# Identity products on TensorE beside the conversion of the first layer's weights, in a fused kernel of top-k attention and two gated layers

## The chip, the cores and the metric

One Trainium2 chip, one of its cores. The metric is the device time of one execution of the program in microseconds, the median of several runs. Five engines take part, each with its own row of instructions that it works off in order: TensorE (PE, with its weight loads as PEld), VectorE (DVE), ScalarE (ACT), GpSimd (POOL), and SyncE (SP), whose row here holds the DMA issues.

## The reference

Attention over 4 x 8 heads of 576 tokens with head size 64, in which each row keeps its 32 largest scores, and behind it two layers on the 2304 tokens of width 512.

```python
scores = scale * np.matmul(q, k.transpose(0, 1, 3, 2))
kth = np.partition(scores, -top_k, axis=-1)[..., -top_k:-top_k + 1]
scores = np.where(scores >= kth, scores, -1000000000.0)
attn = softmax(scores)                                   # 1e-09 is added to the sum
x = np.matmul(attn, v)                                   # heads joined: 2304 x 512
gate = 1.0 / (1.0 + np.exp(-(x @ w_gate)))               # 512 x 1536
x = gate * (x @ w_val) @ w_out                           # 512 x 1536, 1536 x 512
r = np.maximum(x @ w_in, 0.0)                            # 512 x 2048
out = (r * r) @ w_out2                                   # 2048 x 512
```

q, k and v come as float32, the five weights as float64.

## The kernel before

**Tiles.** The 2304 tokens are 18 tiles of 128 rows, grouped in chunks: six of one tile, then six of two. For each chunk the attention of eight heads is computed in units of one head and one tile: scores on PE (line 374), copied out of PSUM by ACT (377), the 32nd largest found by DVE in four rounds of MAX8 and MATCH_REPLACE8 (389, 396), the masked exponentials on ACT (408, 424). The first two chunks then go on in float32: PE transposes the exponentials with a product against a diagonal (472, 483), ACT copies them out (475, 484), PE multiplies with the values (533).

**Weights.** [...] A matrix is cut into blocks of 128 x 512, 12 for each of w_gate, w_val and w_out (wg, wv, wo) and 16 for each of the second layer's (wi, w2). `conv` (586 to 628) takes two blocks at a time: ACT copies the high words (607), DVE shifts them (609), ACT scales the low words (613), the sign comes from DVE (620) or, for one pair in three, from a pass of ACT (616), and POOL adds the low part (623). `scale` (630) sums the squares of a matrix on PE (the gram products of line 640) and derives a power of two from it, and `split` (654) cuts the float32 weight into two float16 ones.

**Layers.** Chunks 0 and 1 run through both layers in float32 (`moe32`, 895): pairs of 128-column slices go through the gate's product and tanh (905, 914), POOL's scaling of it (915), DVE's product g (917), and the accumulation with wo on PE (927), later the second layer (952, 969). All later chunks use three float16 products for one float32 one (`moe_head` and `moe`, lines 747, 787, 851, 872).

**Order.** Nothing of the engines' rows is written out. The program gives each instruction a priority, and a planner that has times of its own for the instructions sets the rows ahead of the run. The loop at 1188 to 1226 gives the weight steps, attention units and layer steps of the first two chunks their due times (`at`, 1167), so that conversion, attention and float32 layers are interleaved. An added instruction can therefore move others, on all engines. A row's instruction waits by semaphores for its inputs and for its buffers, and what stands behind it on its engine waits with it.

**PSUM.** Four pools share its eight banks: ps_s (scores, two banks), ps_t (transposes, two), ps_w (layer products, two) and ps_a (accumulators, two). The first accumulator of the layers is allocated at line 922.

Of the kernel before, what the change touches and what calls it, by code (L numbers as in the profile page):

```python
# [10 lines left out]
F32 = mybir.dt.float32  # L11
# [3 lines left out]
AF = mybir.ActivationFunctionType  # L15
# [3 lines left out]
NOSYNC = mybir.DependencyInfo(mybir.DependencyClass.NoSync, mybir.DependencyReason.DATA)  # L19
DRAM = bass.MemoryType.DRAM  # L20

P = 128
# [22 lines left out]
XP = (0, 1)  # L45
CN = 16
CA2 = 5.0
SM2 = ()
XUP = 1000
DIAG = 2  # L50
# [24 lines left out]
def tile_topk_attention__then__two_moe_layers(  # L75
# [14 lines left out]
    nc = tc.nc  # L90
# [25 lines left out]
    ps_a = ctx.enter_context(tc.tile_pool(name="ps_a", bufs=2, space=PSUM))  # L116
    ps_w = ctx.enter_context(tc.tile_pool(name="ps_w", bufs=2, space=PSUM))

    ident = const.tile([P, P], F32, name="ident")
# [446 lines left out]
    def fetch_to(i):  # L566
        while fetched[0] < len(blocks):
            b = fetched[0]
            spare = b >= len(blocks) - M4RAW
            if b > i and not (b <= i + PREF and (spare or live[0] + 3 <= WSLOTS)):  # L570
                break
            n, kt, fb = blocks[b]
            src = weights[n][kt * P : (kt + 1) * P, fb * 512 : (fb + 1) * 512]
            pool, kw = (mpool, {"tag": "m4", "bufs": M4}) if spare else (wpool, {"tag": "w"})
            if src.dtype == F32:
                t = pool.tile([P, 512], F32, name=f"{n}_r{kt}_{fb}", **kw)
                nc.sync.dma_start(t, src)
            else:
                t = pool.tile([P, 512, 2], U32, name=f"{n}_r{kt}_{fb}", **kw)
                nc.sync.dma_start(t.rearrange("p f t -> p (f t)"), src.bitcast(U32))  # L580
            if not spare:
                live[0] += 1
            raws[(n, kt, fb)] = t
            fetched[0] += 1

    def conv(name, pi):

        pr = pairs_of[name][pi]
        fetch_to(blocks.index((name, *pr[-1])))
        if (name, pi) in CM4:  # L590
            c = mpool.tile([P, 2, 512], F32, tag="m4", bufs=M4, name=f"{name}_c{pi}")
        else:
            c = wpool.tile([P, 2, 512], F32, tag="w", name=f"{name}_c{pi}")
            live[0] += 1
        rs = [raws.pop((name, kt, fb)) for kt, fb in pr]
        ci = c.bitcast(U32)
        wide = weights[name].dtype != F32
        for e, r in enumerate(rs):
            nblk[0] += 1
            if not wide:  # L600
                nc.gpsimd.tensor_copy(c[:, e], r)
            elif YMOD and nblk[0] % YMOD == 0:
                nc.gpsimd.tensor_scalar(
                    c[:, e], r.bitcast(F32)[:, :, 1], REBIAS, 1.0, op0=ALU.mult, op1=ALU.mult
                )
            else:
                nc.scalar.activation(c[:, e], r.bitcast(F32)[:, :, 1], AF.Copy, scale=REBIAS)
        if wide:
            nc.vector.tensor_scalar(ci, ci, 3, None, op0=ALU.logical_shift_left)
            for e, r in enumerate(rs):  # L610
                hi = r[:, :, 1]
                low = r[:, :, 0].bitcast(I32)
                nc.scalar.activation(low, r[:, :, 0], AF.Copy, scale=float(2.0**-29))
                if nblk[0] // 2 % SGN in SGNS:

                    nc.scalar.activation(
                        r.bitcast(F16)[:, :, 1], hi.bitcast(F32), AF.Copy, scale=float(2.0**-60)
                    )
                else:
                    nc.vector.scalar_tensor_tensor(  # L620
                        ci[:, e], hi, 0x80000000, ci[:, e], op0=ALU.bitwise_and, op1=ALU.bitwise_or
                    )
                nc.gpsimd.tensor_tensor(
                    c.bitcast(I32)[:, e], c.bitcast(I32)[:, e], low, op=ALU.add
                )
        live[0] -= sum(blocks.index((name, *b)) < len(blocks) - M4RAW for b in pr)
        for e, (kt, fb) in enumerate(pr):
            flat[(name, kt, fb)] = (c, e)
# [42 lines left out]
    def weight_step(n=1):  # L671
        for _ in range(min(n, len(steps) - nstep[0])):
            name, pi = steps[nstep[0]]
            conv(name, pi)
            nstep[0] += 1
# [328 lines left out]
    def attention():  # L1004
# [62 lines left out]
        def tail(n, after=None):  # L1067
# [3 lines left out]
            if pr.hp == 0 and pr.ci not in xts:  # L1071
# [10 lines left out]
                else:  # L1082

                    small = pr.ci in SM2
                    x = mpool.tile(
# [102 lines left out]
    for ci in PLAIN:  # L1188
        n = 0
        while True:  # L1190
# [29 lines left out]
            else:  # L1220
                at(ta)
                with tc.high_priority(offset=0):
                    if next(att, 1) is None:
                        emitted[0] += 1
                ta += CA if emitted[0] < CN else CA2
        body = None
# [56 lines left out]
```

## Time and profile before

| | us |
|---|---|
| median of 3 runs | 1274.77 (1273.74 to 1278.67) |
| profiled execution | 1270.1 |
| its span, first to last instruction | 1267.8 |
| PE busy in the span | 1171.9 (92%) |
| DVE busy | 956.3 (75%) |
| ACT busy | 830.0 (65%) |
| POOL busy | 844.9 (67%) |

Mean granted clock of TensorE over the span: 0.966. The shares are means over stages with different limits: in the first eighth of the span ACT and DVE are nearly full and PE has gaps, later PE is nearly full, and from about 960 us on it is almost the only busy engine. So a stage has to be read by itself: in which of its parts which engine has no idle time, and what an engine that waits is waiting for.

### The profile page before, as it was taken

To read this page: it belongs to the slowest core of one execution; us is meant where nothing else is said; L and a number is where in the kernel's file an instruction comes from. 1 tells how busy PE (TensorE), PEld (TensorE's weight loads), DVE (VectorE), ACT (ScalarE), POOL (GpSimd) and SP (SyncE) were. 2 spreads that over 40 slices of the span, in tenths; PEclk is the share of its full clock that TensorE was granted. 3 is DMA by queue.
4 is the path that set the end of the run, shared out by engine and by line. 5 is a ranking of instruction groups with operands and counts; after the bars stand their busy time and mean duration, and the time that the engine had idled before them with its cause. 6 is when DMAs were issued, how large, how long until landed. Compare 5 with 4: busy or idle time off the path is not lost.

```text
span 1267.8 us, 30670 instructions
## 1 busy us (share of the span) xinstructions
PE 1171.9 (92%) x11477; PEld 952.5 (75%) x11477; DVE 956.3 (75%) x1965; ACT 830.0 (65%) x1719; POOL 844.9 (67%) x1294
## 2 busy tenths in 40 slices
PE   6657889999889989899998999999999999999998
PEld 5436877987777868779786778877886887787775
DVE  6998789899789868889997788998999969210010
ACT  4998996577676766667766676776676757322122
POOL 1788774488776576777875887797688749515223
PEclk9667999999989999999997999999999999999999
DMA  6988763223354346665667465466544623200000
GB/s 183 366 293 284 259 191 85 57 78 88 109 151 118 95 93 147 147 134 119 146 128 155 99 164 120 119 138 154 105 101 92 126 48 67 55 1 1 18 1 17
DMA packets 243188, 153.92 MB, mean 121 GB/s; under 512 B 193120, under 2 KB 209504, under 8 KB 243040
## 3 DMA queue, kind: packets, MB, share of 16 engines
q1 hardware_dynamic: 243040, 151.97, 47.1%
q8 instruction: 90, 1.47, 0.5%
q14 instruction: 58, 0.48, 0.1%
HBM read 105.51 MB, written 18.09 MB: 97 GB/s over the span
## 4 chain that ended last, share of the span: by engine, by line
PE 62%; DVE 14%; ACT 9%; DMA 7%; POOL 5%; issue 3%; SPq 1%; DVEq 0%; POOLq 0%; ACTq 0%
PE ph L851 11%; PE acc L872 10%; PE pv L747 7%; PE pg L747 7%; PE acc L787 6%; PE sp L374 6%; DVE mx L389 5%; DVE W L396 5%; PE xp L506 2%; PE ph L952 2%; DMA PT<-S 2%; DMA kst<-ks 2%; PE acc L969 2%; PE xp L533 2%; PE qpt L334 1%
## 5 line engine op out<-in xcount | busy, mean ns | idle before, releaser
L389 DVE MAX8 mx<-W 128x8 f32<-128x576 f32 x432 | 327.9, 759 | 11.1
L396 DVE MATCH_REPLACE8 W<-mx,W 128x576 f32<-128x576 f32 x288 | 213.8, 742 | 0.0
L851 PE MATMUL ph<-x,wi_w 128*128 128x256 f16 (+1 forms) x1920 | 190.7, 252 | 4.6 <-ACT x L825 3.6
L872 PE MATMUL acc<-w_w,rh 128*128 128x512 f16 x768 | 181.8, 379 | 2.2 <-POOL rh L864 2.2
L851 PEld LDWEIGHTS <-wi_w 128*128 128x128 f16 x1920 | 156.4, 98 | 30.6 <-issue 5.2
L747 PE MATMUL pv<-xs,wv_w 128*128 128x256 f16 (+1 forms) x1440 | 147.0, 254 | 6.0 <-DVE th L759 4.8
L747 PE MATMUL pg<-xs,wg_w 128*128 128x256 f16 (+1 forms) x1440 | 148.2, 253 | 3.1 <-ACT xs L520 2.2
L374 PE MATMUL sp<-kst,qt 128*128 128x288 f32 x608 | 135.3, 335 | 15.7 <-DMA kst<-ks 8.8
L408 ACT ACTIVATE W<-S,mx 128x576 f32<-128x576 f32 x144 | 111.8, 776 | 51.7 <-DVE mx L389 51.4
L454 POOL TENSOR_TENSOR S<-W,S 128x512 f16<-128x512 f32 x192 | 137.0, 736 | 1.6
L747 PEld LDWEIGHTS <-wv_w 128*128 128x128 f16 x1440 | 117.9, 99 | 22.1 <-issue 9.2
L747 PEld LDWEIGHTS <-wg_w 128*128 128x128 f16 x1440 | 118.6, 99 | 17.4 <-issue 1.0
L377 ACT COPY S<-sp 128x576 f32<-128x576 f32 x144 | 92.0, 639 | 57.3 <-PE sp L374 37.5
L872 PEld LDWEIGHTS <-rh 128*128 128x128 f16 x768 | 72.5, 98 | 74.0 <-POOL rh L864 2.8
L787 PEld LDWEIGHTS <-wo_w 128*128 128x128 f16 x1440 | 117.9, 98 | 12.6 <-issue 0.8
L389 DVE MAX8 mx<-S 128x8 f32<-128x576 f32 x144 | 107.3, 745 | 25.0 <-ACT S L377 25.0
L759 DVE TENSOR_TENSOR th<-pv,th 128x512 f32<-128x512 f32 (+1 forms) x60 | 34.5, 576 | 121.3 <-PE pv L747 113.9
L374 PEld LDWEIGHTS sp<-kst,qt 128*128 128x128 f32 x608 | 92.4, 196 | 27.8 <-DMA kst<-ks 8.0
L452 POOL TENSOR_SCALAR W<-W,rz 128x576 f32<-128x576 f32 x96 | 71.9, 749 | 59.8 <-ACT S L451 57.4
L863 POOL TENSOR_TENSOR r<-r 128x512 f32<-128x512 f32 (+1 forms) x80 | 69.6, 871 | 57.4 <-ACT rh L862 51.8
L451 ACT ACTIVATE S<-W,rz 128x576 f16<-128x576 f32 x96 | 74.2, 774 | 50.4 <-DVE rz L447 47.1
L396 DVE MATCH_REPLACE8 W<-mx,S 128x576 f32<-128x576 f32 x144 | 106.9, 743 | 0.3 <-issue 0.3
(290 smaller groups left out, 2349.6 us busy)
## 6 DMA issues: line engine op xcount, KB each, us to landing
kst<-ks SPq DMA_DIRECT2D x112, 288.0 KB, 3.2
v<-vd SPq DMA_DIRECT2D x32, 320.0 KB, 3.4
qn<-in_q_dram SPq DMA_DIRECT2D x128, 64.0 KB, 2.4
wi_r<-in_moe_w_in_dram SPq DMA_DIRECT2D x16, 512.0 KB, 6.1
w_r<-in_moe_w_out_dram SPq DMA_DIRECT2D x16, 512.0 KB, 4.5
v<-in_v_dram SPq DMA_DIRECT2D x56, 128.0 KB, 2.4
wg_r<-in_moe_w_gate_dram SPq DMA_DIRECT2D x12, 512.0 KB, 6.4
wv_r<-in_moe_w_val_dram SPq DMA_DIRECT2D x12, 512.0 KB, 7.0
```

What stands on the lines that cost most here:

```text
L374: nc.tensor.matmul(sp[:, e, 0:HALF], l, r, start=(x == 0), stop=(x == len(ops) - 1))
L377: nc.scalar.copy(ss.rearrange("p (e s) -> p e s", e=2), sp[:, :, 0:HALF])
L389: m8 = nc.vector.max(mx[:, r], cur)
L396: nc.vector.match_replace(wk, mx[:, r], cur, NEG)
L408: nc.scalar.activation(wk, ss, AF.Prelu, bias=kth, scale=-1.0, alpha=1.0 / BIG)
L451: nc.scalar.activation(pp[:, 0:S], wk, AF.Copy, scale=rz)
L452: nc.gpsimd.tensor_scalar(wk, wk, rz, 1.0, op0=ALU.mult, op1=ALU.mult)
L454: nc.gpsimd.tensor_tensor(pp[:, o : o + e - f], wk[:, f:e], pp[:, f:e], op=ALU.subtract)
L747: nc.tensor.matmul(pp[:, e * N : (e + 1) * N], wblk(wd, a, c, f0, P), xs[:, b_, c, :], start=(e == 0 and n == 0), stop=(n == 3 * KM - 1), ...
L787: nc.tensor.matmul(accs[d // 2][:, (d % 2) * N : (d % 2 + 1) * N], wblk("wo", a, f, d * P, P), gh[:, b_, e * N : (e + 1) * N], start=(f == ...
L851: nc.tensor.matmul(ph[:, e * N : (e + 1) * N], wblk("wi", a, c, f0, P), x2[:, b_, c, :], start=(e == 0 and n == 0), stop=(n == 3 * KM - 1) ...
L872: nc.tensor.matmul(acc2[i][:, 0:DM], gh[:, b_, e * N + i * P : e * N + (i + 1) * P], wblk("w2", a, f, 0, DM), start=(f == 0 and x == 0), s ...
```

## The change

With each block of wg, wv and wo, behind the instruction of ACT that scales its low words, the program asks PE for three float32 products of the 128 x 128 identity with itself. They write one bank of ps_a, 128 columns of it, and nobody reads it. Each product is complete in itself (start and stop), so they accumulate nothing. The first of the three is placed behind ACT's instruction in the planner's order; this is an order only, and at run time PE waits for nothing there, since the identity is there from the start and the bank is written by PE alone.

```diff
+WARM = ("wg", "wv", "wo")
+NWARM = 3
...
+    warm = []
+
     def conv(name, pi):
...
-                nc.scalar.activation(low, r[:, :, 0], AF.Copy, scale=float(2.0**-29))
+                lo = nc.scalar.activation(low, r[:, :, 0], AF.Copy, scale=float(2.0**-29))
+                if name in WARM:
+
+                    if not warm:
+                        warm.append(ps_a.tile([P, 512], F32, tag="acc", name="warm"))
+                    for x in range(NWARM):
+                        mm = nc.tensor.matmul(
+                            warm[0][:, 0:P], ident, ident, start=True, stop=True
+                        )
+                        if x == 0:
+                            tc.add_manual_dep(mm.ins, lo.ins.name, NOSYNC, reason="spread")
```

The 108 products stand in 23 groups of 3, 6 or 9 on PE's row, all ahead of the first accumulation of line 927. No other instruction is added or taken away on any engine, but many change places. Three places follow. Lines of the changed kernel are higher: by 2 up to its line 587, by 4 behind that, by 14 behind the added block.

PE, at the scores of the fifth attention unit (`sp_4`; `tp` and `tq` are transposes of an earlier unit, `qpt` those of queries, `kp` and `kl` the two parts of the keys). Before:

```order
L483 MATMUL tq_0_278<-dg_0_203,W_0_187 64x128
L334 MATMUL qpt_2_338<-ident,qn_2_250 128x128 x2
L472 MATMUL tp_1_346<-dg_1_297,W_1_281 128x128 x4
L374 MATMUL sp_4_445<-kp_2_232,qt_2_0_341 128x288
L374 MATMUL sp_4_445<-kl_2_233,qt_2_0_341 128x288
L483 MATMUL tq_1_352<-dg_1_297,W_1_281 64x128
L374 MATMUL sp_4_445<-kp_2_232,qt_2_0_341 128x288
```

Changed:

```order
L485 MATMUL tq_0_285<-dg_0_203,W_0_187 64x128
L623 MATMUL warm<-ident 128x128 x3
L336 MATMUL qpt_2_357<-ident,qn_2_257 128x128 x2
L474 MATMUL tp_1_365<-dg_1_304,W_1_288 128x128 x4
L376 MATMUL sp_4_476<-kp_2_239,qt_2_0_360 128x288
L376 MATMUL sp_4_476<-kl_2_240,qt_2_0_360 128x288
L485 MATMUL tq_1_371<-dg_1_304,W_1_288 64x128
L623 MATMUL warm<-ident 128x128 x3
L376 MATMUL sp_4_476<-kp_2_239,qt_2_0_360 128x288
```

Two groups of three have come in between, ahead of six of the eight score products.

POOL and DVE, at the end of the float32 gate's first pair (`th_0` is the tanh that line 915 scales, `g_0` its product with the other branch, which the first accumulation reads). POOL before:

```order
L623 TENSOR_TENSOR wo_c_1036<-wo_c_1036,wo_r_0_914 128x512
L623 TENSOR_TENSOR wo_c_1036<-wo_c_1036,wo_r_0_916 128x512
L623 TENSOR_TENSOR wi_c_1072<-wi_c_1072,wi_r_0_928 128x512
L623 TENSOR_TENSOR wi_c_1072<-wi_c_1072,wi_r_0_930 128x512
L915 TENSOR_SCALAR th_0_959<-th_0_959 128x256
L405 TENSOR_SCALAR bs_1_1023<-mx_1_1015 128x1
```

Changed:

```order
L637 TENSOR_TENSOR wo_c_1139<-wo_c_1139,wo_r_0_1005 128x512
L637 TENSOR_TENSOR wo_c_1139<-wo_c_1139,wo_r_0_1007 128x512
L929 TENSOR_SCALAR th_0_1062<-th_0_1062 128x256
L637 TENSOR_TENSOR wi_c_1181<-wi_c_1181,wi_r_0_1025 128x512
L637 TENSOR_TENSOR wi_c_1181<-wi_c_1181,wi_r_0_1027 128x512
L407 TENSOR_SCALAR bs_1_1126<-mx_1_1118 128x1
```

DVE before:

```order
L389 MAX mx_2_1121<-S_2_996 128x8
L609 TENSOR_SCALAR wi_c_1233<-wi_c_1233 128x1024
L396 MATCH_REPLACE W_2_1120<-mx_2_1121,S_2_996 128x576
L620 SCALAR_TENSOR_TENSOR wi_c_1233<-wi_r_0_1032,wi_c_1233 128x512
L620 SCALAR_TENSOR_TENSOR wi_c_1233<-wi_r_0_1034,wi_c_1233 128x512
L917 TENSOR_TENSOR g_0_962<-pg_0_942,th_0_959 128x256
```

Changed:

```order
L391 MAX mx_2_1230<-S_2_1099 128x8
L931 TENSOR_TENSOR g_0_1065<-pg_0_1045,th_0_1062 128x256
L613 TENSOR_SCALAR wi_c_1342<-wi_c_1342 128x1024
L398 MATCH_REPLACE W_2_1229<-mx_2_1230,S_2_1099 128x576
L634 SCALAR_TENSOR_TENSOR wi_c_1342<-wi_r_0_1135,wi_c_1342 128x512
L634 SCALAR_TENSOR_TENSOR wi_c_1342<-wi_r_0_1137,wi_c_1342 128x512
```

The scaling has moved ahead of two additions for wi on POOL, and the product ahead of a shift, a match-replace and two merges on DVE.

ACT, a little later, ahead of the copy of the first transposed block of chunk 1 (`PT_0`). Before:

```order
L424 ACTIVATE W_1_1014,bs_1_1023<-W_1_1014,bs_1_1023 128x576
L607 ACTIVATE wi_c_1247<-wi_r_1_1068 128x512
L613 ACTIVATE wi_r_1_1068<-wi_r_1_1068 128x512
L607 ACTIVATE wi_c_1247<-wi_r_1_1070 128x512
L613 ACTIVATE wi_r_1_1070<-wi_r_1_1070 128x512
L607 ACTIVATE wi_c_1419<-wi_r_1_1229 128x512
L613 ACTIVATE wi_r_1_1229<-wi_r_1_1229 128x512
L475 COPY PT_0_1003<-tp_0_1004 128x512
```

Changed:

```order
L611 ACTIVATE wi_c_1356<-wi_r_1_1177 128x512
L617 ACTIVATE wi_r_1_1177<-wi_r_1_1177 128x512
L174 CAST kp_1_1072<-kpt_1_0_1073 128x512
L174 CAST kp_1_1072<-kpt_1_4_1080 128x64
L611 ACTIVATE wi_c_1356<-wi_r_1_1179 128x512
L617 ACTIVATE wi_r_1_1179<-wi_r_1_1179 128x512
L611 ACTIVATE wi_c_1528<-wi_r_1_1338 128x512
L617 ACTIVATE wi_r_1_1338<-wi_r_1_1338 128x512
L630 ACTIVATE wi_r_1_1338<-wi_r_1_1338 128x512
L611 ACTIVATE wi_c_1528<-wi_r_1_1340 128x512
L617 ACTIVATE wi_r_1_1340<-wi_r_1_1340 128x512
L477 COPY PT_0_1106<-tp_0_1107 128x512
```

The copy of the keys (`kp_1`) has moved between the conversions, and three more conversions of wi, one each of lines 607, 613 and 616 of before, stand ahead of `PT_0` than did. The same three stand behind the tanh of the first pair (line 914) now and stood ahead of it. On PE the transposes that `PT_0` copies stand behind 35 more gram products (640) and four more accumulating products (927) than before, and the five transposes of the keys of chunk 1's second pair of heads have moved from ahead of the first accumulation to behind it.

## Rows read from the trace of the kernel before

**Rows 1.** Page part 2: granted clock of TensorE in 40 slices, tenths.

```profile
PEclk9667999999989999999997999999999999999999
```

**Rows 2.** Windows: length, busy us (count) of PE, PEld, DVE, ACT, POOL, clock, DMA, GB/s.

```profile
20.00:36.00 16.00, 15.06 (x67) 11.81 (x67) 13.92 (x29) 11.94 (x25) 3.83 (x8) 1.00 0.92 298
36.00:109.00 73.00, 42.54 (x198) 32.37 (x199) 67.53 (x108) 72.77 (x133) 62.86 (x56) 0.60 0.90 313
44.00:54.00 10.00, 2.19 (x7) 1.45 (x8) 9.90 (x18) 10.00 (x19) 9.15 (x8) 0.51 1.01 370
54.00:64.00 10.00, 9.86 (x49) 8.02 (x49) 9.66 (x17) 9.93 (x18) 9.83 (x10) 0.50 1.05 378
64.00:69.00 5.00, 1.90 (x11) 1.24 (x11) 4.97 (x8) 5.00 (x11) 3.77 (x4) 0.84 1.04 370
69.00:109.00 40.00, 23.88 (x109) 18.07 (x110) 36.15 (x55) 39.84 (x73) 35.37 (x32) 0.54 0.81 274
109.00:119.00 10.00, 5.27 (x46) 4.96 (x45) 9.93 (x18) 8.35 (x18) 7.72 (x8) 0.99 0.83 293
119.00:123.00 4.00, 4.00 (x22) 3.67 (x22) 4.00 (x10) 2.32 (x5) 3.05 (x4) 0.57 0.86 305
123.00:175.00 52.00, 45.39 (x446) 41.07 (x444) 38.79 (x85) 47.79 (x87) 40.16 (x38) 1.00 0.78 249
```

**Rows 3.** Timeline of PE: start, us, instructions [idle before <-releaser].

```profile
32.27 0.44 PE L374 MATMUL sp<-kp,qt 64*128 64x288 f32 x1
...
32.51 0.44 PE L374 MATMUL sp<-kl,qt 64*128 64x288 f32 x1
...
37.53 0.29 PE L374 MATMUL sp<-kp,qt 64*128 64x288 f32 x1
...
37.65 0.29 PE L374 MATMUL sp<-kl,qt 64*128 64x288 f32 x1
...
55.07 2.08 PE L472 MATMUL tp<-dg,W 128*128 128x128 f32 x8
...
118.93 0.49 PE L927 MATMUL acc<-g,wo_c 128*128 128x128 f32 x2 [4.73 <-DVE g L917]
...
124.97 1.96 PE L640 MATMUL wg_n<-wg_c 128*128 128x128 bf16 x31
...
128.16 2.00 PE L927 MATMUL acc<-g,wo_c 128*128 128x128 f32 x16
```

**Rows 4.** Timeline of ACT, the fifth block's score copy.

```profile
33.47 0.64 ACT L377 COPY S<-sp 128x576 f32<-128x576 f32 x1 [0.19 <-PE sp L374]
```

**Rows 5.** Timeline of ACT at 121 to 125 us.

```profile
120.64 0.68 ACT L613 ACTIVATE wi_r<-wi_r 128x512 int32<-128x512 uint32 x1
124.71 0.59 ACT L475 COPY PT<-tp 128x512 f32<-128x512 f32 x1 [3.39 <-PE tp L472]
```

**Rows 6.** Timeline of DVE, from a shift to product g.

```profile
115.36 1.12 DVE L609 TENSOR_SCALAR wi_c<-wi_c 128x1024 uint32<-128x1024 uint32 x1
...
118.46 0.41 DVE L917 TENSOR_TENSOR g<-pg,th 128x256 f32<-128x256 f32 x1
```

**Rows 7.** Timeline of POOL, two additions and the gate's scaling.

```profile
113.39 2.54 POOL L623 TENSOR_TENSOR wi_c<-wi_c,wi_r 128x512 int32<-128x512 int32 x2 [0.68 <-POOL wo_c L623]
115.90 0.84 POOL L915 TENSOR_SCALAR th<-th 128x256 f32<-128x256 f32 x1
```

**Rows 8.** Chain of waits at 170 to 178 us: start, us, what.

```profile
170.03 1.25 ACT w_r L616
...
171.28 1.05 ACT w_r L613 x2
...
172.34 1.16 ACT w_c L607 x2
...
175.59 2.05 PE acc L927 x16
```


## The prediction

> **What bounds the kernel now.** I read the page's row of granted clocks first, because the change is about TensorE. Three of its 40 slices, the second to the fourth (32 to 127 us), stand at 0.6 to 0.7, and nearly all others at 0.9 or full [rows 1]. So the change can act on one stretch, the one in which ACT, DVE and POOL convert the float64 weights while the first attention blocks run.
>
> Then I cut that stretch where the clock moves [rows 2]. From 36 to 109 us ACT is busy 72.8 of 73 us, at a mean clock of 0.60. PE is busy 42.5 us of the same 73 and idle for 30.5. PE is not the limit here, ACT is. Behind 109 us that changes for a moment: ACT drops to 8.35 of 10 us, PE to 5.27 of 10, and then from 119 to 123 us PE is busy all the time at a clock of 0.57. This seam is where the stage hands over, and where I expect the time to move. After it ACT is nearly full again, 47.8 of 52 us from 123 to 175, and the chain of waits runs over its conversions until PE takes over at 175.6 us [rows 2, 8]. What makes ACT earlier there makes the program's end earlier.
>
> The granted clock has to be read with the pace. From 20 to 36 us the rows give 1.00, yet score products start 0.24 us apart at 32.3 us and 0.12 us apart at 37.6 us [rows 2, 3]. PE ran at half pace until about 37 us; the view seems to have no change of clock to show before its first one.
>
> **The change, part by part.** *The products.* Three weights have 12 blocks each, so there are 36 x 3 = 108 products, 128x128 by 128x128 in f32. Their nearest rows are the kernel's own f32 products of that shape. A pass of line 472 issues four and the trace shows eight instructions, so one product is two. At half clock eight take 2.08 us, 0.26 each; at full clock sixteen take 2.00 us, 0.125 each [rows 3]. A product is 0.5 or 0.25 us, all together 56 or 27. By PE's order 24 stand ahead of the third block's transposes (40 us in the trace of before) and 84 behind.
>
> *Their cover up to 109 us.* If the 84 run at full clock they take 21 us, and PE's own 12.05 + 23.88 = 35.9 us from 44 to 64 and 69 to 109 us, nearly all at half clock, shrink to about 18. PE then needs 42.5 - 18 + 21 = 46 of 73 us and fits under ACT. If nothing raises the clock the products take 44 us, and PE needs 86 of 73: 13 us too many, and ACT would wait for scores and transposes. Which it is hangs on the clock. It rose to a mean of 0.84 from 64 to 69 us, behind ten microseconds with PE busy 9.86; in those five PE was busy 1.90, and behind them the mean is 0.54 [rows 2]. The groups of products stand mostly ahead of instructions that PE waits for, so they fill just such gaps. I take the full clock for most of the stretch and keep 13 us as the upper bound. The gain from a faster clock by itself is bounded by ACT's idle time here, 0.2 us; I take 0.
>
> *The front.* Around the second transposed block stand two groups of three, 6 x 0.5 = 3.0 us ahead of most of the fifth block's scores. PE is busy 15.06 of 16 us there, and ACT's copy of a score had waited 0.19 us for PE [rows 2, 4]. For the scores the delay is real. ACT covers it if it has conversions to do meanwhile, and its new order puts four more instructions ahead of the copy of the fifth score block. Bounds 0 and 3.0 us; I take 0.4, near zero, because ACT is full from 36 us on.
>
> *The seam.* This comes from the rows that move, not from the clock. On POOL the first gate's scaling now stands ahead of two wi_c additions, which took 2.54 us before it; POOL reaches it when these began, at 113.4 instead of 115.9 us [rows 7]. On DVE the product g now stands ahead of a shift, a match-replace and two merges; from the start of that shift to the start of g there are 118.46 - 115.36 = 3.1 us [rows 6]. With its input there by 114, g starts at 115.4, and the first accumulation 3.1 us before the 118.93 of before, where PE had waited 4.7 us [rows 3]. ACT's tanh has three conversions less ahead of it, so it doesn't hold g back. With a gap of under 2 us I also expect the clock to stay up behind it: from 119 to 123 us PE did 4 us of work at 0.57 [rows 2], and at full clock that is about 1.9 us less. PE's lead is then 5.0 us.
>
> What is next late? ACT had waited 3.4 us for the transposes behind those accumulations, from the end of a conversion at 121.3 to 124.7 us [rows 5]. They now stand further back in PE's row, behind eight more accumulating instructions and 35 more gram products (8 x 0.125 and 35 x 0.063 us [rows 3]) and the keys' transposes, so that some 4 of PE's 5 us are spent, and they end about 1 us sooner, at 123.7. But ACT now has three more conversions ahead of its copy, of the kinds that take 1.25, 0.53 and 0.58 us on the chain [rows 8], 2.4 us that it does in what was its wait. It comes to the copy at 121.3 + 2.4 = 123.7 us, just as the transposes end. ACT stands 1.0 + 2.4 = 3.4 us further on, and ACT carries the chain to 175 us.
>
> *Everything behind.* Small pieces are reshuffled on all engines, up to three quarters of PE's program and nearly to the end of ACT's, with the same instructions. I cost that at 0 with a spread of 5 us, about the size of the waits that moved here. The sum: -3.4 + 0.4 = -3.0 us. Against the profiled execution (1270.1 us, span 1267.8) that is 1267.1. That execution lies 4.7 us under the median of the three runs, 1274.8, and I carry the difference over to the median: **1271.8 us**.
>
> [...]
>
> **The rivals.**
> - *The lead is lost behind the seam.* DVE, at 19.6 of 20 us from 44 to 64 us [rows 2], is as full as ACT there; if attention on DVE sets the hand-over at 175 us, ACT's 3.4 us are given back as waits. For it: DVE's load. Against it: DVE is busy only 38.8 of 52 us from 123 to 175 [rows 2]. Time 1275.
> - *The lead grows.* ACT has 52 - 47.8 = 4.2 us of waits left from 123 to 175 us [rows 2]. If PE's 5.0 us lead takes them away too, the sum is -3.4 - 4.2 = -7.6 us: 1267.
> - *The clock pays by itself.* If PE's half-clock work were on the path, its 35.9 + 4.0 us of busy time [rows 2] would fall by half: -20 us, 1255. ACT's 72.8 of 73 us speak against it. [...]
> - *Slower: the products don't bring the clock up.* The change then doesn't do what it says. At 0.5 us a product PE is over-full by 13 us up to 109 us, and every group stands in PE's row ahead of scores and transposes that ACT and DVE need. With the seam's 3.4 us still won the time is 1274.8 + 13 - 3.4 = 1284. It decides once more than about 60 of the 84 run at half clock, which is what fills PE's idle 30.5 us. For it: from 20 to 36 us PE was busy 94% of the time and still at half pace [rows 2, 3]. Against it: the rise at 64 us.
>
> **How the numbers follow.** Forecast 0.52; lead lost 0.14; lead grows 0.17; clock pays 0.04; slower 0.13. About 0.5%, 6.4 us, is what a measurement of this kernel can tell from no change. Faster by more: the growing lead, the paying clock, and 0.03 of the forecast's spread, 0.24. Slower by more: the over-full PE and 0.02 of that spread, 0.15. Within: 0.61. For 8 times in 10 the range runs from 1264 (the growing lead less part of the spread) to 1281 (part of the over-full case). It leaves out the paying clock, the worst of the slower case and the ends of the spread.
>
> **What the next profile would show.** Right: a mean clock above 0.85 from 44 to 109 us, the added products' instructions at about 0.125 us, ACT still without idle time there, the first accumulation at about 116 us, and ACT's wait for the transposes gone. Wrong on the clock: 0.5 in those stretches, and ACT waiting for PE. Wrong on the seam: the first accumulation at 119 us or later. Wrong behind it: the accumulations of 175.6 us no earlier than before, or an end that moves by more than that hand-over does.

## The result and the profile after

The changed kernel takes **1281.4 us** (median of 7 runs, 1277.9 to 1283.2) against 1274.4 us (median of 7) for the kernel before. The ratio is 1.0052, with a 95% interval of 1.0035 to 1.0070. It is slower by half a per cent, about 7 us. The forecast was 1271.8 us, and the range ended at 1281.

The two profiled executions overstate this. The one of before took 1270.1 us, 4.3 us less than its median; the one of after took 1283.1 us, 1.7 us more. Of the 13.0 us between the two traces, 6 are scatter of single executions. So in what follows places are read from traces, and sizes are taken from medians wherever there is one.

What the change says it does, it does. The page's row of clocks, 40 slices of the span, answers to [rows 1]:

```profile
PEclk9889789999999999899999999999999999999999
```

The windows answer to [rows 2]; columns are the stretch, its length, busy us (and count) of PE, PEld, DVE, ACT and POOL, granted clock, DMA share, GB/s:

```profile
36.00:109.00 73.00, 57.71 (x396) 50.10 (x395) 67.88 (x109) 71.89 (x133) 61.82 (x55) 0.84 0.89 311
44.00:54.00 10.00, 5.01 (x25) 3.94 (x26) 9.90 (x16) 10.00 (x20) 9.11 (x9) 0.78 1.00 368
54.00:64.00 10.00, 10.00 (x62) 8.44 (x62) 9.93 (x18) 9.93 (x17) 9.83 (x9) 0.70 1.02 355
64.00:69.00 5.00, 5.00 (x43) 4.69 (x42) 5.00 (x8) 5.00 (x11) 3.76 (x4) 1.00 0.78 266
69.00:109.00 40.00, 30.94 (x218) 26.96 (x218) 36.52 (x59) 38.98 (x72) 34.92 (x31) 0.83 0.81 285
109.00:119.00 10.00, 7.25 (x66) 6.73 (x65) 9.96 (x17) 7.10 (x12) 9.22 (x9) 1.00 0.98 372
119.00:123.00 4.00, 4.00 (x56) 3.91 (x53) 3.25 (x9) 4.00 (x10) 3.06 (x4) 1.00 0.18 42
123.00:175.00 52.00, 41.96 (x366) 37.89 (x366) 39.13 (x79) 46.98 (x84) 37.01 (x36) 0.87 0.74 241
```

From 36 to 109 us the mean clock is 0.84 where it was 0.60. PE is busy 57.7 us instead of 42.5, and ACT still has only 1.1 us of idle time in 73. At the seam the clock is 1.00 from 119 to 123 us, where it was 0.57. The last row turns the other way: from 123 to 175 us PE has the clock at 0.87, where it was 1.00, and is busy 42.0 us instead of 45.4.

In the timeline of PE (start, us, instructions, idle time before and who ended it) the added products run at 2.17 / 18 = 0.12 us at full clock and at 2.45 / 12 = 0.20 where the mean clock is 0.70. The first accumulation, which answers to 118.93 in [rows 3], comes 3.6 us sooner. Behind it PE waits 4.31 us for product g, then does sixteen accumulating instructions in 3.78 us, half pace:

```profile
58.13 2.45 PE L623 MATMUL warm<-ident 128*128 128x128 f32 x12
...
65.02 2.17 PE L623 MATMUL warm<-ident 128*128 128x128 f32 x18
...
115.35 0.49 PE L941 MATMUL acc<-g,wo_c 128*128 128x128 f32 x2 [2.75 <-DVE g L931]
...
147.05 3.78 PE L941 MATMUL acc<-g,wo_c 128*128 128x128 f32 x16 [4.31 <-DVE g L931]
...
180.51 1.30 PE L376 MATMUL sp<-kst,qt 128*128 128x288 f32 x4 [2.83 <-DMA kst<-ks]
...
184.07 3.07 PE L941 MATMUL acc<-g,wo_c 128*128 128x128 f32 x16
```

The last of these rows answers to 175.59 in [rows 8]: the hand-over is 8.5 us later than before in these two traces, although the seam was 3.6 us earlier. Two runs below with the old rows up to there, e1 and e9, have it at 177.15 and 177.26 us, so nearly 2 of the 8.5 us are scatter. ACT's timeline shows what it met on the way:

```profile
118.56 0.78 ACT L426 ACTIVATE W<-W,bs 128x576 f32<-128x576 f32 x1 [2.90 <-POOL bs L407]
...
125.75 0.56 ACT L477 COPY PT<-tp 128x512 f32<-128x512 f32 x1
...
153.19 0.70 ACT L174 CAST kp<-kpt 128x512 fp32r<-128x512 f32 x2 [4.11 <-PE kpt L167]
```

The wait of 3.39 us for the transposes [rows 5] is gone, as forecast. Two new waits of ACT, 2.90 and 4.11 us, have come.

### The profile page after: what moved, and what is told of

Read it like the earlier page. It is cut to its first block, busy times and chain, and to the rows that moved or that the text cites. A ratio compares the mean times of both kernels' runs of the same rounds, so it can differ in the third digit from the quotient of the medians.

```text
span 1281.3 us, 31093 instructions
## 1 busy us (share of the span) xinstructions
PE 1192.0 (93%) x11693; PEld 975.3 (76%) x11693; DVE 962.8 (75%) x1965; ACT 833.7 (65%) x1719; POOL 836.9 (65%) x1294
## 4 chain that ended last, share of the span: by engine, by line
PE 65%; DVE 10%; DMA 7%; POOL 7%; ACT 6%; issue 4%; SPq 2%; POOLq 0%; DVEq 0%; ACTq 0%
PE ph L865 10%; PE acc L886 10%; PE acc L801 8%; PE pg L761 8%; PE pv L761 7%; PE sp L376 6%; DVE mx L391 4%; DVE W L398 3%; PE xp L508 3%; DMA PT<-S 3%; PE ph L966 2%; PE acc L983 2%; PE xp L535 2%; DMA kst<-ks 1%; POOL S L456 1%
## 5 line engine op out<-in xcount | busy, mean ns | idle before, releaser
L376 PE MATMUL sp<-kst,qt 128*128 128x288 f32 x608 | 132.4, 328 | 15.1 <-DMA kst<-ks 9.5
L801 PEld LDWEIGHTS <-wo_w 128*128 128x128 f16 x1440 | 119.4, 99 | 19.7 <-issue 6.3
L773 DVE TENSOR_TENSOR th<-pv,th 128x512 f32<-128x512 f32 (+1 forms) x60 | 34.7, 578 | 123.2 <-PE pv L761 119.4
L801 PE MATMUL acc<-gh,wo_w 128*128 128x256 f16 (+1 forms) x1104 | 105.8, 249 | 2.3 <-POOL gh L777 2.1
```

What stands on the lines that cost most here:

```text
L376: nc.tensor.matmul(sp[:, e, 0:HALF], l, r, start=(x == 0), stop=(x == len(ops) - 1))
L801: nc.tensor.matmul(accs[d // 2][:, (d % 2) * N : (d % 2 + 1) * N], wblk("wo", a, f, d * P, P), gh[:, b_, e * N : (e + 1) * N], start=(f == ...
```

## The experiments

The diff itself has 108 products in it, but the planner's answer to it is much larger. Of PE's 10,669 other instructions 2,192 stand out of the old sequence, of ACT's 1,550 it is 497, and they lie all the way to 1000 us (counted as what is left over when the longest common sequence of the two orders is taken out). So the first question was whether the products or the order cost the time.

To part them, the order of every engine's instructions was written out as a table and held with ordering hints that add no semaphore (`NOSYNC`). The table can be that of before, that of after, or one up to some time and the other behind it:

```diff
-                        if x == 0:
-                            tc.add_manual_dep(mm.ins, lo.ins.name, NOSYNC, reason="spread")
+                        WARMED.append(mm.ins)
...
+ORDER = (
...
+def pin(nc, tc, warm):
...
+    for row in zlib.decompress(base64.b85decode(ORDER)).decode().split("|"):
...
+                ins = rows[x] if x >= 0 else warm[-x - 1]
+                if last is not None:
+                    tc.add_manual_dep(ins, last.name, NOSYNC, reason="pinned")
+                last = ins
...
         tile_topk_attention__then__two_moe_layers(tc, *args)
+        pin(nc, tc, WARMED)
```

The products belong to no result, so leaving them out or adding more changes nothing that is computed. The medians below are each beside 1274.1 to 1274.8 us for the kernel before on the same chip.

| run | products | order | us | ratio to before, 95% |
|---|---|---|---|---|
| e1 | 3 a block | before | 1274.5 | 0.9978 to 1.0012 |
| e2 | none | after | 1285.2 | 1.0054 to 1.0098 |
| e3 | 3 | after to 118 us, then before | 1272.1 | 0.9963 to 1.0000 |
| e4 | 3 | before to 118 us, then after | 1286.9 | 1.0064 to 1.0117 |
| e5 | 3 | after to 140, then before | 1274.0 | 0.9988 to 1.0023 |
| e6 | 3 | after to 190, then before | 1275.7 | 0.9998 to 1.0036 |
| e7 | 3 | after, one exchange undone | 1281.3 | 1.0038 to 1.0085 |
| e8 | none | after to 118, then before | 1273.5 | 0.9989 to 1.0021 |
| e9 | 3 | before to 190, then after | 1281.2 | 1.0036 to 1.0075 |
| e10 | 3 | after to 400, then before | 1278.8 | 1.0024 to 1.0056 |
| e11 | 6 | planner's own, 173 PE rows moved | 1275.1 | 0.9983 to 1.0022 |
| e12 | none | planner's own, 1,692 moved | 1279.0 | 1.0023 to 1.0060 |
| e13 | 2 | planner's own, 1,256 moved | 1282.9 | 1.0051 to 1.0090 |
| e14 | 4 | planner's own, 1,911 moved | 1281.6 | 1.0043 to 1.0080 |
| e15 | none | planner's own, 892 moved | 1270.9 | 0.9962 to 0.9984 |

**Products or order: e1 and e2.** e1 is the diff above with the table of before; e2 has the table of after and

```diff
-WARM = ("wg", "wv", "wo")
+WARM = ()
```

> The 108 products are issued, but every engine's instructions are held to the order of the kernel before by ordering hints (the products stand behind the same PE rows as in the changed kernel). Theory A (the loss is the new order of the rows; the products themselves cost nothing): the first accumulation comes at about 115.5 to 116 us instead of 118.9, the wait of 4.3 us at 143 us is not there, and the time is 1270 to 1275 us. Rival B (the products themselves cost, by PE's time, the clock or what they displace): about 1281 us, as the changed kernel. Rival D (any early gain is lost again behind, whatever the order): within 2 us of the kernel before, 1272 to 1276 us, with the lead of 3 us gone by 250 us.

> The products are left out, and every engine's instructions are held to the order of the changed kernel. Theory A (the order is the loss): slower than before by at least as much as the changed kernel, 1281 to 1286 us, since the clock between 44 and 109 us is at half again and the seam comes 3 to 4 us later as well. Rival B (the products themselves are the loss): about 1274 us, as the kernel before.

e1 is at par with the kernel before, e2 slower by 0.8%. The order is the loss, and the products alone cost nothing that can be measured; nor does holding an order, which e1 does too. (e1's time fits rival D as well, but it made no early lead that could have been lost.) e2's ratio is 0.0024 above that of the change and the intervals overlap, so whether the products give something back under the new order isn't shown. Both runs also missed my numbers for the first accumulation, and both misses say the same thing. It stands so in the timeline of PE, of e1 and then of e2:

```profile
119.38 0.80 PE L941 MATMUL acc<-g,wo_c 128*128 128x128 f32 x2 [5.43 <-DVE g L931]
...
113.74 0.49 PE L941 MATMUL acc<-g,wo_c 128*128 128x128 f32 x2 [3.38 <-DVE g L931]
```

With the old order and the products it stays at 119.4 us, as before. With the new order and no products it comes at 113.7, even sooner than in the changed kernel. The earlier start of the seam is made by the moved rows, and the products are no part of it. They may have one in the pace behind it: in e2 the next pairs of accumulating instructions take 0.73 us each, in the changed kernel 0.44 (the rows stand in the last section). e1's windows, of the same columns as above, show that the clock did rise there and nothing came of it:

```profile
36.00:109.00 73.00, 55.83 (x390) 48.30 (x389) 67.44 (x109) 72.77 (x133) 62.92 (x56) 0.86 0.88 308
```

0.86 instead of 0.60, and ACT is busy 72.77 us, to the hundredth what it was in [rows 2].

**Where in the order: e3, e4, e5, e6.** Four more tables, cut at 118 us (the first accumulation), 140 and 190 us.

> Products as in the changed kernel; every engine holds to the order of the changed kernel for what starts before 118 us and to the order of the kernel before for the rest. Theory A with the loss placed behind the seam (118 to 190 us): 1270 to 1275 us. Rival C (the loss is in the order ahead of the seam, where bs, kn and the conversions were moved too): about 1281 us.

> The reverse of the run before it: products in place, the order of the kernel before for what starts before 118 us, and that of the changed kernel for the rest. Theory A with the loss behind the seam: about 1281 us, with PE waiting some 4 us for the first layer's third gate product near 143 us. Rival C: 1270 to 1275 us.

> Products in place; the changed kernel's order for what starts before 140 us, the order of the kernel before for the rest. It holds the stretch 118 to 140 apart, in which the changed kernel's first row maximum of head 4 (134 us) came 3.3 us late. Theory A1 (most of the loss is the one exchange near 143 us, the accumulation of the third pair put ahead of the fourth pair's products): 1272 to 1275 us. Rival A2 (the loss is made between 118 and 140, where PE's filler rows stand ahead of the work that others wait for): 1278 to 1282 us.

> As the run before it, with the changed kernel's order kept up to 190 us. If the loss is made before 190 us and stays: 1280 to 1283 us, 8 us behind the kernel before at 217 us and to the end. If the rows behind 190 us cost as well (or give back), the difference to 1281.4 us is theirs.

The new order ahead of the seam costs nothing (e3, 1272.1 us; its interval touches 1.0, so a gain of 2 us isn't shown). What follows the seam costs, as theory A has it: e4 loses 12.6 us, more than the 7 expected of it. e5 came out in A1's range and contradicts A2, in which the loss is made up to 140 us. e6 takes in the exchange near 143 us and contradicts A1. Up to 190 us the new order costs 1.6 us in all, with an interval that reaches no change, so most of the 7 us had to lie behind 190 us, in a part that I hadn't read.

**One exchange undone: e7.** The most visible new wait is the 4.31 us at 147 us. In the old order the fourth pair's products stood ahead of that accumulation. e7 is the changed kernel's order with this one move on PE (a line is a run of PE's rows):

```diff
   wv_n<-wv_c x48
-  acc<-g (third pair) x8
   wv_cb<-wv_d,ones
   pg (fourth pair) x5, kpt<-ident,kn, pg x11
+  acc<-g (third pair) x8
   pg (fifth pair) ...
```

> The changed kernel with one move on PE alone: the 8 products of the third pair's accumulation stand behind the fourth pair's products again, as in the kernel before; all else is in the changed kernel's order. Theory A1: the 4.1 us wait of ACT for the transposed keys at 153 us shrinks to about 1 us, and the time falls by 3 to 5 us to 1276 to 1278 us. Rival A2: the wait moves to the column sums that stand behind the same late DVE rows, and the time stays within 1.5 us of 1281.4 us.

The local half of theory A1 came out and the rest did not. PE's timeline of e7, then ACT's row for the keys:

```profile
146.35 0.29 PE L662 MATMUL wv_cb<-wv_d,ones 128*128 128x128 bf16 x1 [4.39 <-DVE wv_d L660]
...
153.21 1.95 PE L941 MATMUL acc<-g,wo_c 128*128 128x128 f32 x16
...
179.12 1.30 PE L377 MATMUL sp<-kst,qt 128*128 128x288 f32 x4 [3.48 <-ACT w_c L612]
...
182.46 2.05 PE L941 MATMUL acc<-g,wo_c 128*128 128x128 f32 x16
```

```profile
149.77 0.70 ACT L175 CAST kp<-kpt 128x512 fp32r<-128x512 f32 x2 [1.59 <-PE kpt L168]
```

ACT's wait falls from 4.11 to 1.59 us, and the accumulation is done at normal pace. PE's wait does not go: it moves to the column sums behind the same late DVE rows (4.39 us), as rival A2 has it, and a wait of 2.83 us at 180 becomes one of 3.48 at 179. The hand-over is 1.6 us sooner, and the median is the same as the changed kernel's, 1281.3 against 1281.4 us. So ACT's wait, which stood out in the trace, was not what the time was lost to; PE's was only moved by this run, not taken away.

**The products again, without pinning: e8 and e11.** e8 is e3 without the products. e11 takes another number of them and leaves the order to the planner:

```diff
-NWARM = 3
+NWARM = 6
```

> Run e3 without its products: the changed kernel's order up to 118 us and the order of the kernel before behind it. If e3's 2 us come from the moved rows alone: 1270 to 1273 us, and the first accumulation no later than with products. If they come from the products (the clock at the seam): 1274 to 1277 us.

> Six products for each block instead of three, nothing pinned: 216 products, but the planner happens to leave the rows nearly as in the kernel before (173 of PE's 10,669 rows stand out of the old sequence, 2,192 in the changed kernel). If the order is the cause: 1271 to 1277 us, like the kernel before, with twice the products. If the products' own time on PE or their effect on the clock is the cause: 1284 us or more.

e8's 1273.5 us lies between the two cases; its ratio is 0.0023 above e3's and the intervals overlap, so nothing follows from the time. Its first accumulation, at 113.98 us in its trace, is no later than e3's. e11 is clear. Twice the products, at par. Its windows:

```profile
36.00:109.00 73.00, 68.36 (x574) 63.34 (x573) 67.02 (x109) 72.83 (x133) 62.01 (x56) 1.00 0.90 321
```

PE is now busy 68.4 of 73 us, the granted clock is 1.00 through the whole stretch, and ACT is as full as before, 72.8 us.

**Behind 190 us: e9 and e10.**

> Products in place; the order of the kernel before for what starts before 190 us, that of the changed kernel behind it. If the rows behind 190 us cost what the runs so far leave for them (1281.4 for the whole of the new order less 1275.7 for the new order to 190), 5 to 6 us: 1278 to 1281 us, with PE idle for about 41 us between 190 and 1000 us where the kernel before has 36.9. If the cost needs the late seam ahead of it: 1274 to 1276 us.

> The changed kernel's order up to 400 us, the order of the kernel before behind it. If the loss behind 190 us is made in one place ahead of 400 us (the accumulation that waits 2.0 us at 283, the gates that wait 5.5 us at 350, the accumulation that waits 2.1 us at 371): 1280 to 1282 us. If it is spread over the rows up to 1000 us: 1276 to 1279 us.

e9 costs 6.8 us with the old order up to 190 us, so the rows behind it cost by themselves. e10 splits them. The steps of the ladder, in differences to before, are: to 118 us -2.2, to 140 -0.1, to 190 +1.6, to 400 +4.4, all +7.0. Behind the seam that is 2.1, 1.7, 2.8 and 2.6 us, each known to about 3 us. None of the four steps stands out. e10's median lies in the range of the spread case, but its interval (1277.5 to 1281.6 us) reaches that of the other, so that the loss has no one place is likely and not shown. Counted from the other end (e9 +6.8, e4 +12.6) the parts are somewhat larger, so they don't simply add.

The hand-over tells the two parts of the loss apart in another way. This is its row in PE's timeline of e6, then of e9:

```profile
183.69 2.05 PE L941 MATMUL acc<-g,wo_c 128*128 128x128 f32 x16
...
177.26 2.05 PE L941 MATMUL acc<-g,wo_c 128*128 128x128 f32 x16 [2.56 <-DVE g L931]
```

e6 reaches it as late as the changed kernel, and that execution took 1277.2 us; e9 reaches it 6.4 us sooner and took 1280.6. What follows the start of this row, up to the time of the same execution, is 1095.7 us in mean in the six traces with the old rows behind 190 us (1092.5 to 1099.9) and 1101.9 us in the five with the new ones (1097.1 to 1107.4). The ranges overlap by e8's trace, but the 6 us between the means fit e9's median.

PE is the fullest engine there, and part of the loss shows as its idle time. The windows from 190 to 1000 us of the kernel before, e1, e6 (old order) and of after, e2, e9 (new order), in this sequence:

```profile
190.00:1000.00 810.00, 773.12 (x8328) 635.12 (x8329) 715.68 (x1504) 567.17 (x1239) 594.00 (x1005) 0.99 0.51 119
190.00:1000.00 810.00, 773.74 (x8333) 636.57 (x8332) 713.84 (x1500) 568.28 (x1241) 593.70 (x1005) 0.98 0.50 118
190.00:1000.00 810.00, 772.81 (x8308) 634.08 (x8308) 711.39 (x1491) 565.70 (x1236) 590.53 (x998) 0.99 0.50 117
190.00:1000.00 810.00, 768.67 (x8273) 630.60 (x8273) 713.23 (x1489) 567.40 (x1232) 584.05 (x996) 0.99 0.50 117
190.00:1000.00 810.00, 767.97 (x8173) 629.74 (x8173) 701.76 (x1471) 556.85 (x1215) 577.04 (x987) 0.97 0.51 115
190.00:1000.00 810.00, 769.96 (x8238) 630.70 (x8238) 711.74 (x1487) 563.43 (x1227) 584.95 (x994) 0.98 0.50 117
```

810 less the first number is PE's idle time: 36.9, 36.3 and 37.2 us with the old rows, 41.3, 42.0 and 40.0 with the new. The eleven kernels with one of the two orders in this whole stretch give 36.9 in mean for the old one (33.1 to 40.1, six traces, e8 the highest) and 40.8 for the new (39.7 to 42.0, five). The 3.9 us between the means are a balance: single waits of some us come and others go (the kernel before has one of 4.8 us there that the changed kernel has too, at 5.5). These are four that came, in PE's timeline of the changed kernel:

```profile
283.15 2.05 PE L941 MATMUL acc<-g,wo_c 128*128 128x128 f32 x16 [2.00 <-DVE g L931]
...
370.89 2.50 PE L801 MATMUL acc<-gh,wo_w 128*128 128x128 f16 x22 [2.08 <-POOL gh L777]
...
531.75 1.08 PE L167 MATMUL kpt<-ident,kn 128*128 128x128 f32 x4 [3.65 <-DMA kn<-in_k_dram]
...
573.50 1.50 PE L801 MATMUL acc<-gp,wo_w 128*128 128x128 f16 x24 [3.10 <-ACT ob L904]
```

**Other reshuffles: e12 to e15.** If the order is the cause, an order changed without any product should cost too. Both e12 and e15 are the kernel before with one number of its plan changed (the lead in due time of the first block's steps), e13 and e14 are the change with other numbers of products. The edits, in the sequence of the runs:

```diff
-MUP = 200.0
+MUP = 201.0
...
-NWARM = 3
+NWARM = 2
...
-NWARM = 3
+NWARM = 4
...
-MUP = 200.0
+MUP = 195.0
```

> No products: the kernel before with one number of its planner changed (MUP from 200 to 201, the lead in due time of the first block's steps), which moves 1,692 of PE's 10,669 rows out of the old sequence. If the old order is one that is better than its neighbours, any reshuffle costs: 1278 to 1285 us. If a reshuffle is a draw with both signs: 1268 to 1280 us. If order matters nothing: 1273 to 1275 us.

> Two products for each block, nothing pinned; the planner moves 1,256 of PE's 10,669 rows out of the old sequence (2,192 with three products). Theory D (nearly any reshuffle of this planner's order costs, more with more rows): 1276 to 1280 us. Theory E (this one reshuffle was unlucky, others come out on both sides): 1268 to 1275 us in at least one of these three runs.

> Four products for each block, nothing pinned; 1,911 of PE's rows out of the old sequence. Theory D: 1278 to 1284 us. Theory E: 1268 to 1275 us in at least one of these three runs.

> No products; the kernel before with the same planner's number moved the other way (MUP from 200 to 195), 892 of PE's rows out of the old sequence. Theory D: 1275 to 1279 us. Theory E: 1268 to 1275 us in at least one of these three runs.

With no product at all e12 loses 4.5 us, about two thirds of what the change loses. e13 and e14 lose 8.1 and 6.8. e15 gains 3.9 us (0.9973, 0.9962 to 0.9984) and has the lowest ratio measured here, ahead of both orders. So theory E holds by the letter, reshuffles come out on both sides; but of the five that move more than 8% of PE's rows, this change among them, four lose 4.5 to 8 us. The one that moves 2%, e11, loses nothing. Beyond that the loss doesn't follow the count, as theory D has it: e13 moves the fewest rows of the four and loses most. Nor are the four independent: counted in the same way, e12 and e14 differ from each other in only 758 of PE's rows. Five orders are too few to say how often one is better, and why e15's is better was not followed up: its profiled execution took 1278.3 us, 7 us more than its median, and can't speak for it.

## Why the prediction was wrong

- **The products' pace and their cover: right.** 0.12 us an instruction at full clock, ACT nearly without idle time from 36 to 109 us (1.1 of 73), and no cost in e1 and e11. The clock from 44 to 109 us was 0.82 in mean (0.78, 0.70, 1.00 and 0.83 in the four windows), a little under the 0.85 that I named. The front cost next to nothing: in e1, with the rows as before, the row maximum that stood at 84.26 us in the trace of before stands at 84.54.
- **No gain from the clock itself: right, and shown.** e11 has the clock at 1.00 for 73 us and gains nothing (0.9983 to 1.0022). The rival in which the clock pays by itself put PE's half-clock work on the path and had 20 us to win; e11 won none. From 36 to 109 us ACT is busy 72.8 of 73 us with the clock at 0.60 (before) and at 1.00 (e11): it is ACT that the kernel waits for there, not PE.
- **The seam: right on PE in size and cause, short on ACT.** The first accumulation came 3.6 us sooner (forecast 3.1), the clock stayed up behind it, and ACT's wait of 3.39 us went. That the moved rows bring the first accumulation forward, not the clock, is what e2 shows. One cost was overlooked. The POOL rows that let the gate's scaling pass keep the attention's `bs` behind them:

```profile
113.92 0.40 POOL L929 TENSOR_SCALAR th<-th 128x256 f32<-128x256 f32 x1
114.29 3.00 POOL L637 TENSOR_TENSOR wi_c<-wi_c,wi_r 128x512 int32<-128x512 int32 x2
117.25 1.27 POOL L407 TENSOR_SCALAR bs<-mx 128x1 f32<-128x1 f32 x1
```

  ACT waits for that `bs` until 118.56 us, 2.90 us. So the copy of the transposes came at 125.75 us instead of the 123.7 I forecast, 1.0 us later than in the trace of before. With the three conversions more ahead of it (2.4 us) ACT stood about 1.4 us further on there, not the 3.4 of the sum.
- **ACT carries the lead to 175 us: wrong in the change, borne out under another order.** In the change the accumulation of 175.59 us came at 184.07. In e3, where the old order follows the seam, the first accumulation is 4.4 us sooner than in the trace of before and the one of 175.59 us is 2.4 sooner, both in single executions:

```profile
114.54 0.49 PE L941 MATMUL acc<-g,wo_c 128*128 128x128 f32 x2 [2.27 <-DVE g L931]
...
173.16 2.05 PE L941 MATMUL acc<-g,wo_c 128*128 128x128 f32 x16 [2.54 <-DVE g L931]
```

- **"Everything behind ... I cost that at 0 with a spread of 5 us": this is the step that failed.** The new rows behind 190 us cost 6.8 us by themselves (e9, 1.0036 to 1.0075). All that follows the seam costs some 9 us: e3, with the old rows there, takes 1272.1 us, the change with the new ones 1281.4. By the ladder 3.8 of these fall up to 190 us, where ACT was to carry its lead, and 5.4 behind it. e3 is close to the 1271.8 us that was forecast, but that may be chance: e8, the same order without the products, takes 1273.5 us, and neither interval excludes no change. So the gain of the sum isn't shown, and its last term, put at 0, was mis-sized by most. I had read "the same instructions in another sequence" as a term without a sign. In four of the five larger reshuffles run here it had one, a loss of 4.5 to 8 us. The reason may be that the old plan is one of the better ones of its kind, so that most of its neighbours are worse; that is argued from the five, not shown. Which rows make the loss stays open.
- **The rivals.** The slower one that I priced (the clock does not rise, PE over-full) did not happen. The one in which the lead is lost behind the seam comes closest, but it had DVE set the hand-over and stopped at no change. Nothing in the list had the order itself as a cost, though the difference of the two orders was there to be counted: a fifth of PE's rows, a third of ACT's.

How a row that moves can hold its engine up, the trace of the changed kernel shows in one place. ACT waited 4.11 us at the row of 153.19 us, with conversions behind it that it ran only afterwards, from 153.78 us on. By e7 this wait was not what the time was lost to, so that a moved row costs time in this way was not shown here.

## What to carry to other kernels

Where a planner sets the order, count first how many rows an edit moves. If they are many, expect the reshuffle to have a price of its own, more often a loss: here four of five that moved a twelfth or more of PE's rows lost 0.4 to 0.7%, one gained 0.3%, and the count didn't tell how much. To learn whether an edit itself is good, hold the order and change only the edit, as e1 and e2 do; otherwise two plans are compared, and the edit is not measured. And a faster clock on an engine that wasn't waited for paid nothing here: from 36 to 109 us it went from 0.60 (before) to 1.00 (e11), and the time stayed the same (0.9983 to 1.0022).

## What was not expected of the hardware

- The pace at the seam went with the wait just ahead of it. These are pairs of accumulating instructions behind the first one, in PE's timeline of the changed kernel, where the wait was 2.75 us, and of e2, where it was 3.38:

```profile
116.07 0.44 PE L941 MATMUL acc<-g,wo_c 128*128 128x128 f32 x2
...
115.28 0.73 PE L941 MATMUL acc<-g,wo_c 128*128 128x128 f32 x2
```

  e2's pairs stay at 0.73 us until 117 us, and from 119 to 123 its clock is back at 1.00. Behind waits of 4.73 us (before) and 5.43 us (e1, at 0.86 in mean from 36 to 109 us) the clock from 119 to 123 us was 0.57 and 0.50. At 147 us, behind 4.31 us of waiting, the changed kernel's sixteen instructions took 3.78 us instead of 2.00.
- Single executions of one program lie far apart. The kernel before took 1267.4 to 1279.7 us in 24 runs, e3 1265.6 to 1276.1 in 12. A difference of 5 us between two traces says nothing of where a change acts until medians say the same.
